# Windowed attention with two MLPs in fp32: when the weights' conversion steps of the 512-token block are traced, and what GpSimd does first

## The chip, the cores and the metric

One core of a Trainium2 chip runs the whole program. The metric is the time of the program on the device in microseconds (us), the median of several runs. The profile is one more execution of the same program, recorded by the hardware profiler.

## The reference

A windowed attention with 4 batches, 8 heads, 576 positions and 64 columns a head, then two MLPs over its 2304 tokens (512 columns, 2048 hidden ones). Only the first MLP matters here:

```python
h = x @ w_in
g = np.where(h >= 1, h, np.where(h <= -1, 0.0, (h + 1) ** 2 / 4))
x = g @ w_out
```

The weights come as float64 and the products have to be nearly exact, so each float32 operand is split into a high and a low part and each product is three matmuls (low x high, high x low, high x high).

## The kernel before

**Stages.** The attention of the first tokens comes first. Then the first MLP goes over the tokens in blocks of 512, 256 and four times 384 tokens, while the attention of later tokens runs in between ("ticks"). The second MLP ends the program. This case is about the first of the blocks, with 512 tokens, which runs from 46.6 us to about 160 us.

**A block.** `run_block` goes over 16 chunks f of 128 hidden columns. `first` (L672) makes h of a chunk in one PSUM bank with 12 matmuls of 512 columns. `activate` makes g of it. `second` (L725) multiplies g with w_out, again 12 matmuls, and is two chunks late (LAG = 2), so that TensorE works on chunk f-2 while g of chunk f is made. From chunk 2 on h has a single PSUM bank, tag h0 (L894 and L895).

**The activation** takes two forms in this block. Even chunks: L712 on VectorE reads h, L713 on ScalarE squares, L714 on VectorE reads h again. Odd chunks: L705 on ScalarE reads h, L706 on ScalarE squares, L707 on VectorE reads h again. Then `split_hi` (L151, ScalarE, "cast of g") makes g's high part and `split_lo` (L158, GpSimd) its low part.

**The weights' conversion.** Float64 weights become float32 with integer arithmetic. The weights of chunk n (tile `raw`) go through three parts:

- part 1, `conv1`: L194 on ScalarE takes the absolute value into tile `m`, L197 on GpSimd leaves the sign in place of the upper words, L198 on ScalarE shifts the lower words
- part 2, `conv2`: L205 on VectorE shifts `m` and sets the sign (it needs L197), L212 on VectorE adds the lower words (it needs L198)
- part 3, `conv3`: L151 on ScalarE makes the high part `wa` ("cast of the weights"), L158 on VectorE the low part; then tile `m` is free. There are two tiles `m`.

Parts 1 and 2 of weights 0 to 2 and part 3 of weights 0 and 1 are traced before the block. The rest is traced by `hook`, which `run_block` calls twice in a chunk: after `first` and `activate` (after = 0), and after `second` (after = 1).

**What sets the order.** A scheduler orders the instructions of each engine by the order of tracing and its own estimate of when each can start; every engine then runs its queue strictly in order. `tc.issue_after(x)` keeps what is traced inside behind x, if it is on the same engine as x. Only SyncE, which issues the DMAs, runs in the order of tracing.

Of the kernel before, what the change touches and what calls it, by code (L numbers as in the profile page):

```python
# [9 lines left out]
F32 = mybir.dt.float32  # L10
# [6 lines left out]
ALU = mybir.AluOpType  # L17
# [13 lines left out]
LO = dict(q="pool", v="pool", x="dve", x_whole="dve", g="pool", g_tail="dve", g2="dve", x2="dve")  # L31
# [11 lines left out]
def tile_window_attention_two_mlps(  # L43
# [76 lines left out]
    def keep_busy(bank, n):  # L120


        for a in range(0, n, 2 * P):
            nc.tensor.matmul(bank[:, a:a + 2 * P], zeros[:, :P], zeros, start=True, stop=True, skip_group_check=True)
# [22 lines left out]
    engines = {"act": nc.scalar, "dve": nc.vector, "pool": nc.gpsimd, "any": nc.any}  # L147

    def split_hi(eng, hi, x):
        if eng == "act":  # L150
            nc.scalar.copy(hi, x)  # L151
        elif eng == "pool":
            nc.gpsimd.tensor_scalar(out=hi, in0=x, scalar1=1.0, scalar2=1.0, op0=ALU.mult, op1=ALU.mult)
        else:
            engines[eng].tensor_copy(hi, x)

    def split_lo(eng, lo, x, hi):
        engines[eng].tensor_tensor(out=lo, in0=x, in1=hi.bitcast(F32), op=ALU.subtract)  # L158

    class Weights:
# [51 lines left out]
        def conv3(self, f):  # L214
            del self.raw[f]
            m = self.m.pop(f)
            hl = wpool.tile([P, 2, 2, PIECE], F32R, tag=f"w{f}", name=f"w{self.nm}{f}")
            split_hi("act", hl[:, 0], m)
            split_lo("dve", hl[:, 1], m, hl[:, 0])
            self.hl[f] = hl  # L220
# [466 lines left out]
    class Mlp1(Mlp):  # L687
# [12 lines left out]
        def activate(self, ps, n):  # L700


            r, g = self.tiles()
            if n == N0 and self.n_first % 2 == 0:
                nc.scalar.activation(out=r[:, :n], in_=ps[:, :n], func=AF.Relu, bias=0.5, scale=0.5)  # L705
                nc.scalar.activation(out=r[:, :n], in_=r[:, :n], func=AF.Square)  # L706
                nc.vector.scalar_tensor_tensor(out=r[:, :n], in0=ps[:, :n], scalar=1.0, in1=r[:, :n],  # L707
                                               op0=ALU.max, op1=ALU.min)
                split_hi(HI["g"], g[:, 0, :n], r[:, :n])
                split_lo(LO[self.g_lo], g[:, 1, :n], r[:, :n], g[:, 0, :n])  # L710
                return g
            nc.vector.tensor_scalar(out=r[:, :n], in0=ps[:, :n], scalar1=-1.0, scalar2=1.0, op0=ALU.max, op1=ALU.min)  # L712
            self.square = nc.scalar.activation(out=r[:, :n], in_=r[:, :n], func=AF.Square, bias=0.5, scale=0.5)  # L713
            self.larger = nc.vector.tensor_tensor(out=r[:, :n], in0=ps[:, :n], in1=r[:, :n], op=ALU.max)  # L714
            split_hi(HI["g"], g[:, 0, :n], r[:, :n])
            split_lo(LO[self.g_lo], g[:, 1, :n], r[:, :n], g[:, 0, :n])
            return g

        def second(self, acc, g, f, n, first, last):
# [118 lines left out]
    W1 = Weights("a", w_in1, w_out1, cpool, True)  # L838
# [12 lines left out]
    def run_block(mlp1, j, part, hook):  # L851
        for f in part:
            chunks.run(mlp1, j, f, part, j, lambda: hook(f, 0), lambda: hook(f, 1), att.behind)

    with ExitStack() as actx:
        mlp1 = Mlp1(W1, blocks1, rpool, GG)
        raw = actx.enter_context(tc.tile_pool(name="raw", bufs=2))
        proc = actx.enter_context(tc.tile_pool(name="proc", bufs=2))
        work = actx.enter_context(tc.tile_pool(name="work", bufs=2))
        dist = actx.enter_context(tc.tile_pool(name="dist", bufs=1)).tile([P, H, 2 * P], BF16, tag="dist", name="dist")  # L860
        zeros = actx.enter_context(tc.tile_pool(name="zeros", bufs=1)).tile([P, 2 * P], BF16, tag="zeros", name="zeros")
        att = Attention(raw, proc, work, XX)

        nc.vector.memset(zeros, 0.0)
        att.clear(range(4))

        nc.scalar.copy(minus_odd, nc.const_aps.tensor(0.0, [P, 1], F32))
        bank = psum.tile([P, BANK], F32, tag="h1", name="busy")
        for _ in range(WARM_UP):
            keep_busy(bank, BANK)  # L870
        make_consts()
        for vt in att.vts:
            nc.gpsimd.memset(vt[:, :, 0:2 * D + 2:2 * D + 1], 1.0)
        att.more_loads(5)

        for t in range(unit_steps[0] + unit_steps[1] + LAG_D + 1):
            att.tick()
            if t < 2:
                with att.behind():
                    att.clear(range(4 + 2 * t, 6 + 2 * t))  # L880
            if t in LOAD_AT:
                W1.load()
            if t in CONV_AT:
                with att.behind(), att.behind_exp():
                    W1.conv_part(CONV_AT[t])

        def spread(ticks):

            slots, att0 = 2 * KF, att.t

            def hook(f, after):
                k = 2 * f + after + 1
                W1.load()
                if f == 1:  # L894
                    mlp1.tags = ("h0",)  # L895
                with att.behind(), att.behind_exp():
                    for part in ((2,) if after else (3, 1)):
                        W1.conv_part(part)
                while att.t < att0 + min(ticks, -(-ticks * k // (slots - 2))):
                    att.tick()  # L900

            return hook

        def even(ticks):

            start = att.t

            n = KF - 1  # L910
            extra = max(0, ticks - n)

            def hook(f, after):
                due = min(n, f + 1) + -(-extra * min(n, f + after) // n)
                while att.t < start + min(ticks, due):
                    att.tick()

            return hook

        mlp1.tags = ("h0", "t2")  # L920
        att.open = False
        ticks = unit_steps[2] + unit_steps[3]
        att.make_tables()
        run_block(mlp1, 0, FULL, spread(ticks))
        assert W1.n_parts == [KF] * 3
        for j in range(1, len(blocks1) - 1):
            ticks = sum(unit_steps[:needs[j + 1]]) + LAG_C_SPLIT - att.t
            run_block(mlp1, j, FULL, even(ticks))
# [246 lines left out]
    for m, blk, f, part, g in chunks.pend:  # L1175
        assert f == KF - 1
        t0, n = m.blocks[blk]
# [181 lines left out]
```

## Time and profile before

| what | us |
|---|---|
| median of 3 runs | 947.78 |
| lowest and highest run | 946.98, 948.83 |
| the profiled execution, its own time | 950.93 |
| its span, first to last instruction | 949.1 |
| TensorE busy in the span | 931.2 |

In the profile PE is TensorE, DVE is VectorE, ACT is ScalarE, POOL is GpSimd and SP is SyncE. L712 is line 712 of the kernel. The granted TensorE clock was 0.998 of full speed over the span. Names such as `wa` or `g` are the program's tiles with the buffer numbers left out.

### The profile page before, as it was taken

Reading aid. Unit: us, or ns where it says so; the run is one execution under the profiler, and the core shown is the slowest. Engines: PE = TensorE matmul, PEld = TensorE weight load, DVE = VectorE, ACT = ScalarE, POOL = GpSimd, SP = SyncE. Lnnn points to the kernel's source line nnn. Section 1 sums busy time; section 2 is a strip of 40 time slices with the busy share of each in tenths; the row PEclk is TensorE's granted clock in tenths of the full one; section 3 lists DMA queues with packets and bytes.
Section 4 is the critical chain, followed back from the end, with each engine's and each line's share of the span. In section 5 each row is a group of like instructions: output and inputs, shape, how many; then the busy total and the mean of one; then the engine's idle time right before and its main releaser. Section 6 shows DMA issues by size and latency. Waiting matters only on the chain.

```text
span 949.1 us, 16367 instructions
## 1 busy us (share of the span) xinstructions
PE 931.2 (98%) x5299; PEld 855.1 (90%) x5299; DVE 653.0 (69%) x1706; ACT 534.4 (56%) x1325; POOL 299.5 (32%) x559
## 2 busy tenths in 40 slices
PE   9999999999999999999999999999999999999998
PEld 7776878999999999999999899999999898988987
DVE  5788785787677677667644899968557777644443
ACT  6887875776666566666534785635333334422232
POOL 2144555887668676777710000000000000000000
PEclk9999999999999999999999999999999999999999
DMA  6675412322222212322008762004264644544431
GB/s 199 205 241 182 164 37 73 96 79 73 74 64 71 81 43 71 91 64 62 1 35 278 251 222 92 1 20 170 78 211 160 239 167 149 174 121 113 122 111 66
DMA packets 92644, 112.73 MB, mean 119 GB/s; under 512 B 8721, under 2 KB 70417, under 8 KB 92561
## 3 DMA queue, kind: packets, MB, share of 16 engines
q1 hardware_dynamic: 92560, 111.71, 36.9%
q8 instruction: 42, 0.69, 0.3%
q14 instruction: 42, 0.34, 0.1%
HBM read 87.56 MB, written 24.12 MB: 118 GB/s over the span
## 4 chain that ended last, share of the span: by engine, by line
PE 74%; DVE 6%; ACT 3%; issue 1%; DMA 1%; POOL 0%; ACTq 0%; SPq 0%; POOLq 0%; DVEq 0%
PE h L672 21%; PE acc L778 21%; PE acc L725 14%; PE y L1260 7%; PE x L1260 5%; PE r L563 3%; PE s L419 2%; PE t L478 1%; DMA rawb<-w_out 1%; DVE kl L399 1%; DVE r L712 1%; DVE ma L212 1%; DVE r L714 1%; DVE x L158 1%; ACT r L713 1%
## 5 line engine op out<-in xcount | busy, mean ns | idle before, releaser
L672 PE MATMUL h<-x,wa 128*128 128x384 f32 (+2 forms) x1152 | 224.4, 341 | 4.9 <-DVE r L714 3.3
L778 PE MATMUL acc<-wb,g 128*128 128x512 f32 x861 | 222.2, 393 | 0.0
L725 PE MATMUL acc<-g,wa 128*128 128x384 f32 (+2 forms) x1152 | 221.9, 339 | 0.0
L672 PEld LDWEIGHTS h<-x,wa 128*128 128x128 f32 x1152 | 191.6, 189 | 16.8 <-DVE r L714 7.4
L725 PEld LDWEIGHTS acc<-g,wa 128*128 128x128 f32 x1152 | 191.7, 189 | 6.3 <-DVE g L158 0.2
L778 PEld LDWEIGHTS acc<-wb,g 128*128 128x128 f32 x861 | 159.4, 188 | 24.9
L151 ACT CAST g<-r 128x384 fp32r<-128x384 f32 (+2 forms) x192 | 98.1, 511 | 68.9 <-DVE r L1207 37.6
L158 POOL TENSOR_TENSOR g<-r,g 128x384 fp32r<-128x384 f32 (+2 forms) x80 | 88.2, 1103 | 57.1 <-ACT g L151 46.6
L158 DVE TENSOR_TENSOR g<-r,g 128x384 fp32r<-128x384 f32 x112 | 62.3, 556 | 41.8 <-ACT g L151 41.4
L713 ACT ACTIVATE r<-r 128x384 f32<-128x384 f32 (+2 forms) x88 | 45.1, 514 | 70.2 <-DVE r L712 70.0
L496 POOL TENSOR_SCALAR_AFFINE_SELECT tt<-dist 128x256 fp32r<-128x256 f32 (+1 forms) x176 | 77.0, 457 | 19.8 <-DVE dist L491 15.3
L712 DVE TENSOR_SCALAR r<-h 128x384 f32<-128x384 f32 (+2 forms) x88 | 47.5, 540 | 41.8 <-PE h L672 33.7
L672 PE MATMUL h<-x,wb 128*128 128x384 f32 x384 | 72.6, 336 | 0.0
L672 PEld LDWEIGHTS h<-x,wb 128*128 128x128 f32 x384 | 68.2, 188 | 2.6
L453 ACT ACTIVATE p<-p,sm 128x128 f32<-128x128 f32 (+2 forms) x134 | 56.7, 429 | 23.9 <-DVE sm L449 23.6
L714 DVE TENSOR_TENSOR r<-h,r 128x384 f32<-128x384 f32 (+2 forms) x88 | 47.8, 544 | 23.5 <-ACT r L713 21.6
L1205 ACT ACTIVATE r<-u 128x384 f32<-128x384 f32 x32 | 16.8, 525 | 56.2 <-DVE u L1269 56.2
L563 PEld LDWEIGHTS r<-tt,vs 128*128 128x128 f32 x304 | 45.1, 189 | 3.5 <-POOL tt L496 1.3
L401 POOL TENSOR_TENSOR qs<-qr,qs 128x256 fp32r<-128x256 f32 (+2 forms) x64 | 39.5, 618 | 26.6 <-ACT qs L398 14.5
L563 PE MATMUL r<-tt,vs 128*128 128x128 f32 (+3 forms) x304 | 44.8, 262 | 1.6 <-POOL tt L496 0.9
L1260 PE MATMUL y<-wb,w 128*128 128x384 f32 x192 | 38.7, 336 | 0.0
L399 DVE SCALAR_TENSOR_TENSOR kl<-kr,kh 128x256 fp32r<-128x256 f32 (+3 forms) x64 | 38.4, 599 | 0.0
(169 smaller groups left out, 1569.2 us busy)
## 6 DMA issues: line engine op xcount, KB each, us to landing
w<-wd SPq DMA_DIRECT2D x88, 256.0 KB, 2.7
rawa<-w_in SPq DMA_DIRECT2D x16, 512.0 KB, 4.8
rawa<-w_out SPq DMA_DIRECT2D x16, 512.0 KB, 5.8
rawb<-w_in SPq DMA_DIRECT2D x16, 512.0 KB, 4.1
rawb<-w_out SPq DMA_DIRECT2D x16, 512.0 KB, 5.0
wd<-sum SPq DMA_DIRECT2D x32, 256.0 KB, 2.1
wd<-wb SPq DMA_DIRECT2D x24, 256.0 KB, 2.8
out<-o SPq DMA_DIRECT2D x17, 256.0 KB, 2.3
```

The lines of the kernel that those rows point to most:

```text
L151: nc.scalar.copy(hi, x)
L158: engines[eng].tensor_tensor(out=lo, in0=x, in1=hi.bitcast(F32), op=ALU.subtract)
L453: self.exp = nc.scalar.activation(out=pt[:, :nk], in_=pt[:, :nk], func=AF.Exp, bias=sm[:, 0:1], scale=-1.0, accum_out=None if u.whole else ...
L496: nc.gpsimd.affine_select(out=u.tt[:, :, s0 + s, :m], in_=both, compare_op=ALU.is_ge, fill=0.0, base=-1 + s, pattern=[[0, 2], [sign, m]], ...
L563: nc.tensor.matmul(u.r[:, qo:qo + nq], u.vs[:, j, c, :, :].rearrange("p a d -> p (a d)"), u.tt[:, part].rearrange("p s q -> p (s q)")[:, s ...
L672: nc.tensor.matmul(ps[:, :n], self.W.w_in(a, c, f), self.x_chunk(x, b, c, n), start=(k == 0), stop=(k == 3 * KC - 1))
L712: nc.vector.tensor_scalar(out=r[:, :n], in0=ps[:, :n], scalar1=-1.0, scalar2=1.0, op0=ALU.max, op1=ALU.min)
L713: self.square = nc.scalar.activation(out=r[:, :n], in_=r[:, :n], func=AF.Square, bias=0.5, scale=0.5)
L714: self.larger = nc.vector.tensor_tensor(out=r[:, :n], in0=ps[:, :n], in1=r[:, :n], op=ALU.max)
L725: nc.tensor.matmul(acc[i][:, o * n:(o + 1) * n], self.W.w_out(a, f)[:, e * P:(e + 1) * P], g[:, b, :n], start=(first and k == 0 and o == 0 ...
L778: nc.tensor.matmul(acc[t][:, :DM], g[:, b, tg * P:(tg + 1) * P], self.W.w_out(a, f), start=(first and k == 0), stop=(last and k == 2))
L1260: nc.tensor.matmul(ps[:, :N2], w[:, a, c * P:(c + 1) * P], self.x.operand(k, c, b), start=(start and n == 0), stop=(n == 5), skip_group_ch ...
```

## The change

`split_lo` returns its instruction, and `activate` keeps that of g's low part as `g_low`. What `hook` traces is held behind `g_low` on GpSimd, which concerns the sign (L197) alone. The parts are traced at other places: from chunk 1 on, the first call of a chunk f has part 2 of weights f+2 and then part 1 of weights f+3, and the second call has part 3 of weights f+2. Before, the first call had part 3 of weights f+2 and part 1 of weights f+3, and the second call part 2 of weights f+3.

```diff
     def split_lo(eng, lo, x, hi):
-        engines[eng].tensor_tensor(out=lo, in0=x, in1=hi.bitcast(F32), op=ALU.subtract)
+        return engines[eng].tensor_tensor(out=lo, in0=x, in1=hi.bitcast(F32), op=ALU.subtract)
...
                 split_hi(HI["g"], g[:, 0, :n], r[:, :n])
-                split_lo(LO[self.g_lo], g[:, 1, :n], r[:, :n], g[:, 0, :n])
+                self.g_low = split_lo(LO[self.g_lo], g[:, 1, :n], r[:, :n], g[:, 0, :n])
                 return g
...
             split_hi(HI["g"], g[:, 0, :n], r[:, :n])
-            split_lo(LO[self.g_lo], g[:, 1, :n], r[:, :n], g[:, 0, :n])
+            self.g_low = split_lo(LO[self.g_lo], g[:, 1, :n], r[:, :n], g[:, 0, :n])
             return g
...
                 W1.load()
                 if f == 1:
                     mlp1.tags = ("h0",)
-                with att.behind(), att.behind_exp():
-                    for part in ((2,) if after else (3, 1)):
-                        W1.conv_part(part)
+                with att.behind(), att.behind_exp(), tc.issue_after(mlp1.g_low.ins):
+                    for part in (3,) if after else (3, 1) if f == 0 else (2, 1):
+                        if not (after and f == 0):
+                            W1.conv_part(part)
```

The order of instructions differs from before on TensorE, VectorE, ScalarE and GpSimd, from chunk 0 or 1 to chunk 15 of this block; behind it, and on SyncE everywhere, it is the same. Three places follow. In the names, `rawa`, `ma` and `wa` with a number are the weights of that chunk; a number behind an underscore only tells buffers apart.

GpSimd, the signs of weights 8 to 10 and the low parts of g of chunks 4 to 7 (`r_1071`, `r_1129`, `r_1204`, `r_1275`), before:

```order
L158 TENSOR_TENSOR g_85<-r_1071,g_85 128x512
L197 TENSOR_SCALAR rawa8_936<-rawa8_936 128x1024
L441 MEMSET p1_115 128x64
L158 TENSOR_TENSOR g_85<-r_1129,g_85 128x512
L441 MEMSET p0_114 128x64
L197 TENSOR_SCALAR rawa9_997<-rawa9_997 128x1024
L158 TENSOR_TENSOR g_85<-r_1204,g_85 128x512
L197 TENSOR_SCALAR rawa10_1077<-rawa10_1077 128x1024
L441 MEMSET p2_116 128x64
L158 TENSOR_TENSOR g_85<-r_1275,g_85 128x512
```

The same stretch now, where the chunks 4 to 7 are `r_1069`, `r_1127`, `r_1202` and `r_1273`:

```order
L158 TENSOR_TENSOR g_85<-r_1069,g_85 128x512
L197 TENSOR_SCALAR rawa7_863<-rawa7_863 128x1024
L441 MEMSET p1_115 128x64
L158 TENSOR_TENSOR g_85<-r_1127,g_85 128x512
L197 TENSOR_SCALAR rawa8_934<-rawa8_934 128x1024
L441 MEMSET p0_114 128x64
L158 TENSOR_TENSOR g_85<-r_1202,g_85 128x512
L197 TENSOR_SCALAR rawa9_995<-rawa9_995 128x1024
L441 MEMSET p2_116 128x64
L158 TENSOR_TENSOR g_85<-r_1273,g_85 128x512
```

The sign of weights 9 stood behind the low part of chunk 5 and now stands behind that of chunk 6; the signs of weights 8 and 10 move by one chunk in the same way.

VectorE, behind the last activation step of chunk 7 (`r_1275`) and around that of chunk 8 (`r_1329`), before:

```order
L707 SCALAR_TENSOR_TENSOR r_1275<-h_1262,r_1275 128x512
L205 SCALAR_TENSOR_TENSOR ma10_1286<-ma10_1286,rawa10_1077 128x1024
L449 ISA p1_115,sm28_1_1312<-s28_1_1310,dist_98 128x192
L449 ISA sm28_1_1312 128x1
L212 ISA ma10_1286<-rawa10_1077,ma10_1286 128x2048
L712 TENSOR_SCALAR r_1329<-h_1316 128x512
L527 TENSOR_SCALAR rec27_1346<-r26_1219 128x4
L449 ISA p2_116,sm29_0_1364<-s29_0_1362,dist_98 128x128
L449 ISA sm29_0_1364 128x1
L158 TENSOR_TENSOR wa10_1337<-ma10_1286,wa10_1337 128x1024
L714 TENSOR_TENSOR r_1329<-h_1316,r_1329 128x512
```

The same stretch now, with chunk 7 as `r_1273` and chunk 8 as `r_1327`:

```order
L707 SCALAR_TENSOR_TENSOR r_1273<-h_1260,r_1273 128x512
L449 ISA p1_115,sm28_1_1310<-s28_1_1308,dist_98 128x192
L449 ISA sm28_1_1310 128x1
L527 TENSOR_SCALAR rec27_1343<-r26_1216 128x4
L528 RECIPROCAL rec27_1343<-rec27_1343 128x4
L158 TENSOR_TENSOR wa9_1300<-ma9_1212,wa9_1300 128x1024
L529 TENSOR_TENSOR y27_1344<-r26_1216,rec27_1343 128x256
L205 SCALAR_TENSOR_TENSOR ma10_1283<-ma10_1283,rawa10_1075 128x1024
L712 TENSOR_SCALAR r_1327<-h_1314 128x512
L212 ISA ma10_1283<-rawa10_1075,ma10_1283 128x2048
L714 TENSOR_TENSOR r_1327<-h_1314,r_1327 128x512
```

L205 of weights 10 stood right behind L707 of chunk 7, with its sign behind the low part of chunk 6; now it stands right ahead of L712 of chunk 8 and its sign behind the low part of chunk 7. L212 now stands between L712 and L714.

ScalarE, from the square of chunk 9 (`r_1407`) to the cast of g, before:

```order
L706 ACTIVATE r_1407<-r_1407 128x512
L194 ACTIVATE ma12_1418<-rawa12_1210 128x1024
L198 ACTIVATE rawa12_1210<-rawa12_1210 128x1024
L151 CAST g_85<-r_1407 128x512
L151 CAST x_78<-x27_1422 128x192
```

The same stretch now (`r_1405`):

```order
L706 ACTIVATE r_1405<-r_1405 128x512
L151 CAST x_78<-x27_1419 128x192
L453 ACTIVATE p1_115<-p1_115,sm30_0_1432 128x128
L151 CAST wa11_1448<-ma11_1337 128x1024
L151 CAST g_85<-r_1405 128x512
```

The conversion of weights 12 no longer stands ahead of the cast of g; the cast of weights 11 does.

## Rows read from the trace of the kernel before

**Rows 1.** The page, busy us by engine, share of the span, instructions.

```profile
PE 931.2 (98%) x5299; PEld 855.1 (90%) x5299; DVE 653.0 (69%) x1706; ACT 534.4 (56%) x1325; POOL 299.5 (32%) x559
```

**Rows 2.** Window: length, busy us of PE, PEld, DVE, ACT, POOL; clock, DMA.

```profile
57.00:160.00 103.00, 99.00 (x493) 78.87 (x493) 81.53 (x155) 78.92 (x144) 53.88 (x54) 1.00 0.43 140
```

**Rows 3.** Waits of TensorE from 57 to 160 us: total, times, longest.

```profile
PE s L419 <- DVE sm L449: 1.1, 2, 0.7
PE h L672 <- DVE r L707: 1.0, 1, 1.0
...
PE h L672 <- DVE r L714: 0.5, 1, 0.5
```

**Rows 4.** Groups by line and shape, 57 to 160 us: busy us, mean ns | idle before.

```profile
L725 PE MATMUL acc<-g,wa 128*128 128x512 f32 x168 | 44.9, 403 | 0.0
L672 PE MATMUL h<-x,wa 128*128 128x512 f32 x168 | 44.3, 403 | 1.9 <-DVE r L707 1.0 <-DVE r L714 0.5 <-DVE sm L456 0.3
...
L212 DVE CUSTOM_DVE_ANT_0 ma<-rawa,ma 128x2048 uint16<-128x2048 uint16 x13 | 22.9, 1765 | 0.3
L197 POOL TENSOR_SCALAR rawa<-rawa 128x1024 f32<-128x1024 f32 x12 | 16.1, 1342 | 14.4 <-ACT ma L194 14.4
...
L151 ACT CAST wa<-ma 128x1024 fp32r<-128x1024 f32 x13 | 13.6, 1044 | 2.4 <-DVE ma L212 1.0 <-DVE rec L527 0.7 <-DVE sm L457 0.7
L151 ACT CAST g<-r 128x512 fp32r<-128x512 f32 x16 | 9.9, 620 | 3.8 <-DVE r L707 2.6 <-DVE r L714 1.1
L707 DVE SCALAR_TENSOR_TENSOR r<-h,r 128x512 f32<-128x512 f32 x8 | 5.5, 684 | 5.6 <-ACT r L706 5.6
L712 DVE TENSOR_SCALAR r<-h 128x512 f32<-128x512 f32 x7 | 4.8, 684 | 1.6 <-PE h L672 1.6
```

**Rows 5.** Timeline of TensorE: first matmuls of h in chunks 4, 14 and 15.

```profile
75.22 1.67 PE L672 MATMUL h<-x,wa 128*128 128x512 f32 x6
...
148.60 3.00 PE L672 MATMUL h<-x,wa 128*128 128x512 f32 x12 [0.32 <-DVE sm L456]
...
154.11 2.91 PE L672 MATMUL h<-x,wa 128*128 128x512 f32 x12
```

**Rows 6.** Timelines of ScalarE, GpSimd and VectorE around that wait, start, us.

```profile
82.73 0.62 ACT L151 CAST g<-r 128x512 fp32r<-128x512 f32 x1
...
83.43 2.04 POOL L158 TENSOR_TENSOR g<-r,g 128x512 fp32r<-128x512 f32 x1 [0.38 <-ACT g L151]
85.43 2.13 POOL L197 TENSOR_SCALAR rawa<-rawa 128x1024 f32<-128x1024 f32 x1
...
84.36 2.19 DVE L212 CUSTOM_DVE_ANT_0 ma<-rawa,ma 128x2048 uint16<-128x2048 uint16 x1
...
87.59 1.23 DVE L205 SCALAR_TENSOR_TENSOR ma<-ma,rawa 128x1024 uint32<-128x1024 uint32 x1 [0.77 <-POOL rawa L197]
88.95 1.23 DVE L212 CUSTOM_DVE_ANT_0 ma<-rawa,ma 128x2048 uint16<-128x2048 uint16 x1
90.10 0.68 DVE L707 SCALAR_TENSOR_TENSOR r<-h,r 128x512 f32<-128x512 f32 x1
```

**Rows 7.** Waits of VectorE from 57 to 160 us: total, times, longest.

```profile
DVE ma L205 <- POOL rawa L197: 4.5, 6, 1.5
```

**Rows 8.** Single lines, 50 to 160 us: duration in ns, minimum/median/maximum.

```profile
L158 POOL TENSOR_TENSOR g<-r,g x16: 1285/1494/2207, 57.5 to 159.9; 128x512 fp32r<-128x512 f32 x16
L158 DVE TENSOR_TENSOR wa<-ma,wa x14: 1207/1225/1226, 52.6 to 146.7; 128x1024 fp32r<-128x1024 f32 x14
...
L197 POOL TENSOR_SCALAR rawa<-rawa x13: 1104/1149/2132, 53.7 to 140.6; 128x1024 f32<-128x1024 f32 x13
L205 DVE SCALAR_TENSOR_TENSOR ma<-ma,rawa x13: 1194/1225/2324, 54.9 to 141.8; 128x1024 uint32<-128x1024 uint32 x13
L212 DVE CUSTOM_DVE_ANT_0 ma<-rawa,ma x13: 1212/1980/2320, 56.6 to 143.1; 128x2048 uint16<-128x2048 uint16 x13
L194 ACT ACTIVATE ma<-rawa x13: 1127/1142/1161, 52.4 to 139.4; 128x1024 f32<-128x1024 f32 x13
```

## Prediction

> **What bounds the kernel now.** I read the busy line first. TensorE is busy 98% of the span [rows 1], so time can come only from its idle stretches, or be lost by new ones. Then the program order of both kernels: they differ only inside the 512-token block of the first MLP, and SyncE's DMA queue is the same in both. So I asked the windows for that block. From 57 us (where the orders part) to 160 us (where the block ends) TensorE is busy 99.0 of 103.0 us [rows 2]: 4.0 us idle, which is the most that any reordering can win. The time that is named goes to few causes: TensorE waits 1.1 us for attention scores, 1.0 us for VectorE's last activation step L707 and 0.5 us for its twin L714 [rows 3].
>
> Why those: from chunk 2 on, h has one PSUM bank. The first matmuls of chunk k+1 (I write h(k+1)) may start only when VectorE has read h(k) for the last time, in L714 (even chunks) or L707 (odd ones). TensorE fills the time with second matmuls (L725) of two chunks earlier and with attention. The block holds 168 + 168 matmuls of 512 columns in these 103 us [rows 4], that is 14 chunks, so TensorE needs 99.0 / 14 = 7.07 us a chunk. If the path from one L714/L707 to the next is longer than 7.07 us, it sets the pace and not TensorE.
>
> The longest single stop, 1.0 us for L707 [rows 3], shows such a path. It is the L707 of chunk 5, at 90.10 us. Ahead of it in VectorE's queue stood L205, which waited for GpSimd's sign (end 85.43 + 2.13 = 87.56, L205 at 87.59), then L212, then L707 [rows 6]. The sign itself stood behind g's low part on GpSimd. Over the block L205 waits 6 times, 4.5 us, for signs [rows 7].
>
> **The change part by part.** Nothing is added or removed: each engine has as many instructions as before. Three things move.
>
> 1. *Signs.* From chunk 5 on, sign k+4 stood behind g's low part of chunk k; now it is sign k+3. Seen from the weights, a sign comes one chunk later on GpSimd. By itself it costs nothing there: GpSimd's wait of 14.4 us in front of signs [rows 4] is the cover.
>
> 2. *Shift and add.* L205 and L212 of weights k+2 now stand right ahead of or between L712 and L714 (before L707) of chunk k, for every k from 1 to 13. In the old order chunks 3, 4, 5 and 6 are tied like this, and chunk 10 as well; elsewhere from chunk 7 on the sign had a whole chunk of slack.
>
> 3. *ScalarE.* The low-part conversion of g gives up its place behind L194/L198 and often stands behind the weights' cast wa instead.
>
> Items 1 and 2 together make a closed path: L714/L707 of chunk k-1, cast of g, g's low part on GpSimd, the sign, L205, L212, L714/L707 of chunk k. Its length from the rows: cast of g 0.62 [rows 4], g's low part alone 1.28 (the minimum), sign 1.15, L205 1.23, L212 1.21 (its minimum) [rows 8], L712 0.68 for even k, and L707 0.68 (L714, over as many columns, is taken alike) [rows 4]. Even: 6.85; odd: 6.17. On one engine a follower starts 0.08 before its predecessor's printed end (88.95 + 1.23 = 90.18, L707 at 90.10), and a hop between engines takes 0.03 (the 87.59 above) to 0.08 (cast of g ends 82.73 + 0.62 = 83.35, GpSimd starts 83.43) [rows 6]. With four or five of the one and three of the other a link loses about 0.19. Bare links, then, are 6.7 and 6.0 us: under 7.07.
>
> What stands in the way on these engines is on top. (a) The low part of the weights (L158, 1.22 us) stands between the sign and L707/L714 in VectorE's queue in the links into chunks 4 and 5, and in the links into 6, 7 and 9 it becomes ready just when the sign starts on GpSimd. Does it then run beside the sign, or wait it out? L205 and L212 took up to 2.32 us, and the pairs of rows show why: g's low part (83.43) and L212 (84.36) finish one after the other, 85.47 and 86.55, and the next sign ends at 87.56 [rows 6]. The low part of the weights itself never took over 1.23 us [rows 8], but never met a GpSimd instruction that had started before it either. Its form is that of L205 (two SBUF operands), so I let it wait: +1.22 in five links, 6.1 us. If it ran beside the sign, the three links 6, 7 and 9 would save about 1.1 each, 3.3 us; that is the lower bound of this term.
> (b) In the links into chunks 8, 10, 11, 12 and 13 the cast of the weights (1.04 [rows 4]) stands ahead of the cast of g on ScalarE. It is released by L212, 0.68 before the link begins, so it delays g by 0.36; and the low part that it releases then holds g's low part for 1.22 - 0.62 = 0.60. About 0.9 a link, 4.5 us. Two links have an attention score row more, 0.5 together.
>
> Sum of the ten links from chunk 3 to chunk 13: 5 x 6.85 + 5 x 6.17 = 65.1, less 1.9, plus 6.1, 4.5 and 0.5: 74.3 us. Before, h(4) to h(14) took 148.60 - 75.22 = 73.38 us [rows 5], in which, counted in the orders, the old one has 118 second matmuls and the new one 116; at 0.24 each (12 take 2.91 [rows 5]) that leaves 72.9. So the path loses 1.4 us there. TensorE's own 70.7 us lie under it.
>
> At the start something comes back: L714 of chunk 0 no longer stands behind L205, so the 0.5 us wait for it [rows 3] goes; ScalarE's L194 now ahead of the first cast of g gives about 0.2 of it back. Behind chunk 13 no weights are left, and h(15) follows as before (154.11 [rows 5]). The buffers of the converted weights are two, so L194 of weights n+2 now waits for the low part of weights n, half a chunk ahead of it: ScalarE time off the path, which I cost at nothing; its price if it isn't covered is the second rival's.
>
> Sum: +1.4 - 0.3, taken as **+1.3 us**. The profiled execution took 950.93 us with a span of 949.1; its span would be 950.4. The median of the runs, 947.78, lies 3.15 below it; the forecast is 947.78 + 1.3 = 949.1.
>
> One rule speaks on the term that I chose. The Trainium skill, "SBUF — State Buffer", section "Who interferes with whom", says that a VectorE instruction with two SBUF inputs and a GpSimd instruction that reads SBUF exclude each other, and the second to issue fully blocks. For L212 against g's low part the trace agrees (2.19 us in place of 1.23, in the pair above). For the low part of the weights no row here shows it; by the rule the sum is +1.3 us, without it -2.0.
>
> **The rivals.** *A, the path is covered, faster.* The low part runs beside the sign or gets in ahead of it; then no link of (a) past chunk 5 is longer than 7.07, and L212 mostly runs alone: 13 times at 1.21 in place of 1.77 [rows 4], 7 us of VectorE that serve the activations. For: L205's 4.5 us of waiting is real and its cure is this order. Against: the links into 4 and 5 keep the low part. Time: 947.78 - 2.0 = 945.8, and with every idle microsecond gone 943.8.
>
> *B, ScalarE lengthens the path, slower.* In the new order L194 or L198 stands ahead of L713, L706 or the cast of g in most chunks. ScalarE is busy 78.92 of 103 us [rows 2], so it often has no gap. I counted none of these. If in three of the ten links one such conversion (1.14 each [rows 8]) lands inside the path, it adds 3.4 us: 949.1 + 3.4 = 952.5. It decides from the point where the path is longer than 7.07 a chunk; below that it costs nothing.
>
> *C, the reordering moves waits only.* TensorE's idle 4.0 us come out again elsewhere: 947.8. That the change does not do what it says is ruled out by the order itself.
>
> **How the numbers follow.** A measurement of this kernel can tell about 0.2%, 1.9 us, from no change. Forecast 0.44, with its own range 947.3 to 950.9 ((a) and (b) are 10.6 us together, which I hold known to about a sixth, 1.8 either way); A 0.24; B 0.20; C 0.12. Faster by over 0.2% is A: 0.24. Slower is B and the upper part of the forecast, above 949.7 (0.16): 0.36. The rest, 0.40, is within 0.2%. For 8 in 10 the range takes in the better part of A and of B: 945.0 to 953.0.
>
> **What would show it.** Right: TensorE's waits for L714 and L707 grow to several us, in chunks 8 to 13 above all; L205's waits for the sign grow or stay although L212 falls to about 1.2 us; the low part of the weights shows instances near 2 us; h(4) comes a little earlier than 75.22 us and h(14) later than 148.60. Wrong: L205 waits for almost no sign, and TensorE's idle time between 57 and 160 us is under 2 us (A); or ScalarE conversions stand in the chain of waits ahead of the cast of g (B).

## The result, and the profile after

| | before | after |
|---|---|---|
| median, us | 947.54 (4 runs) | 953.22 (4 runs) |
| lowest and highest run, us | 946.98, 948.83 | 952.02, 953.69 |
| the profiled execution, own time and span, us | 950.93, 949.1 | 953.69, 952.0 |

The change is **slower**: the ratio after to before is 1.0057, with a 95% interval from 1.0044 to 1.0069, which is 5.4 us (4.2 to 6.5). The forecast was 949.1 us, +1.3, with 945.0 to 953.0 us for 8 in 10; the measured median, 953.22, lies 0.2 us above the upper end.

The busy line of the page after, which answers to [rows 1], hardly moves:

```profile
PE 929.7 (98%) x5299; PEld 854.1 (90%) x5299; DVE 648.7 (68%) x1706; ACT 535.3 (56%) x1325; POOL 303.1 (32%) x559
```

The window from 57 to 160 us of after, which answers to [rows 2], shows where the time goes. TensorE is now idle 9.0 us there, not 4.0:

```profile
57.00:160.00 103.00, 94.04 (x468) 75.10 (x467) 76.99 (x150) 76.62 (x140) 57.08 (x53) 1.00 0.41 133
```

The waits of TensorE in the same stretch of after (in total, times, longest) answer to [rows 3]:

```profile
PE h L672 <- DVE r L714: 3.9, 4, 1.2
PE h L672 <- DVE r L707: 3.8, 6, 1.0
```

1.5 us of waits for VectorE's last activation steps have become 7.7 us, ten of them in one block. The wait of VectorE that answers to [rows 7]:

```profile
DVE ma L205 <- POOL rawa L197: 18.5, 12, 2.8
```

So L205 now waits for nearly every sign. The groups by form of after, 57 to 160 us, answer to [rows 4]:

```profile
L158 POOL TENSOR_TENSOR g<-r,g 128x512 fp32r<-128x512 f32 x15 | 22.7, 1517 | 42.3 <-ACT g L151 31.5 <-issue 10.8
L197 POOL TENSOR_SCALAR rawa<-rawa 128x1024 f32<-128x1024 f32 x13 | 19.2, 1478 | 0.0
L158 DVE TENSOR_TENSOR wa<-ma,wa 128x1024 fp32r<-128x1024 f32 x13 | 17.2, 1321 | 3.3 <-ACT wa L151 3.1
L212 DVE CUSTOM_DVE_ANT_0 ma<-rawa,ma 128x2048 uint16<-128x2048 uint16 x13 | 16.6, 1280 | 0.0
```

L212 fell from 1765 to 1280 ns a piece, as, in all but one instance (2.04 us), it no longer meets g's low part, and GpSimd's 14.4 us of idle time in front of signs is gone: the sign stands right behind g's low part every time. L212 costs VectorE 6.3 us less (22.9 against 16.6), and yet TensorE lost 5.0.

TensorE's timeline of after, first matmuls of h in chunks 4 and 14 (in [rows 5] 75.22 and 148.60):

```profile
74.56 1.66 PE L672 MATMUL h<-x,wa 128*128 128x512 f32 x6 [1.04 <-DVE r L707]
...
151.89 0.96 PE L672 MATMUL h<-x,wa 128*128 128x512 f32 x3 [0.79 <-DVE r L707]
```

From h(4) to h(14) it takes 77.33 us, where it took 73.38. The block's last chunk follows, and the next block's first matmul comes at 163.93 us in place of 159.57, 4.4 us later. Behind that the orders are the same; the distance grows by another 0.5 us up to 250 us and then stays near 4.9 us to 500 us.

**One link of the path.** From L714 of chunk 6 to L707 of chunk 7 in after, ScalarE, GpSimd, VectorE and TensorE:

```profile
97.28 0.68 DVE L714 TENSOR_TENSOR r<-h,r 128x512 f32<-128x512 f32 x1
98.00 0.62 ACT L151 CAST g<-r 128x512 fp32r<-128x512 f32 x1 [0.89 <-DVE r L714]
98.77 1.30 POOL L158 TENSOR_TENSOR g<-r,g 128x512 fp32r<-128x512 f32 x1 [4.31 <-ACT g L151]
99.95 1.23 DVE L158 TENSOR_TENSOR wa<-ma,wa 128x1024 fp32r<-128x1024 f32 x1 [0.65 <-ACT wa L151]
100.03 2.10 POOL L197 TENSOR_SCALAR rawa<-rawa 128x1024 f32<-128x1024 f32 x1
102.17 1.23 DVE L205 SCALAR_TENSOR_TENSOR ma<-ma,rawa 128x1024 uint32<-128x1024 uint32 x1 [1.00 <-POOL rawa L197]
103.43 1.23 DVE L212 CUSTOM_DVE_ANT_0 ma<-rawa,ma 128x2048 uint16<-128x2048 uint16 x1
104.57 0.68 DVE L707 SCALAR_TENSOR_TENSOR r<-h,r 128x512 f32<-128x512 f32 x1
...
105.31 0.72 PE L672 MATMUL h<-x,wa 128*128 128x512 f32 x2 [0.50 <-DVE r L707]
```

It is the forecast's closed path, step by step, with no gap over 0.15 us. The low part of the weights started 0.08 us ahead of the sign, and the sign took 2.10 us in place of 1.15: of the 1.15 us that the low part still had to run, 0.95 came on top of the sign, so that the two ran nearly one after the other. The link takes 104.57 - 97.28 = 7.29 us, and TensorE, done early, waits the last 0.50.

### The profile page after: what moved, and what is told of

It reads as the page before. It is cut to its first block, busy times and chain, and to the rows that moved or that the text cites. A ratio compares the mean times of both kernels' runs of the same rounds, so it can differ in the third digit from the quotient of the medians.

```text
span 952.0 us, 16357 instructions
## 1 busy us (share of the span) xinstructions
PE 929.7 (98%) x5299; PEld 854.1 (90%) x5299; DVE 648.7 (68%) x1706; ACT 535.3 (56%) x1325; POOL 303.1 (32%) x559
## 4 chain that ended last, share of the span: by engine, by line
PE 74%; DVE 5%; ACT 2%; issue 2%; DMA 1%; POOL 1%; SPq 0%; ACTq 0%; POOLq 0%; DVEq 0%
PE h L672 21%; PE acc L778 21%; PE acc L725 14%; PE y L1261 7%; PE x L1261 5%; PE r L563 3%; PE s L419 2%; PE t L478 1%; DVE kl L399 1%; DVE r L712 1%; DMA rawb<-w_out 1%; DVE r L714 1%; DVE x L158 1%; DMA x2r<-x2d 0%; ACT vs L151 0%
## 5 line engine op out<-in xcount | busy, mean ns | idle before, releaser
L712 DVE TENSOR_SCALAR r<-h 128x384 f32<-128x384 f32 (+2 forms) x88 | 47.5, 540 | 39.4 <-PE h L672 31.5
L714 DVE TENSOR_TENSOR r<-h,r 128x384 f32<-128x384 f32 (+2 forms) x88 | 47.8, 544 | 23.9 <-ACT r L713 22.2
L401 POOL TENSOR_TENSOR qs<-qr,qs 128x256 fp32r<-128x256 f32 (+2 forms) x64 | 40.2, 630 | 27.0 <-ACT qs L398 15.1
L399 DVE SCALAR_TENSOR_TENSOR kl<-kr,kh 128x256 fp32r<-128x256 f32 (+3 forms) x64 | 39.0, 609 | 0.0
```

Source lines behind the costliest of these rows:

```text
L399: nc.vector.scalar_tensor_tensor(out=u.kl[:, :nk], in0=u.kr[:, :nk], scalar=unit, in1=u.kh[:, :nk].bitcast(F32), op0=ALU.mult, op1=ALU.sub ...
```

## The experiments

Two theories went to the chip first. **Theory 1**: the closed path through the sign sets the pace. **Theory 2**: ScalarE's new order (rival B of the forecast) lengthens each activation. The time of each run is a median; the ratio is to the kernel before on the same chip, with its 95% interval. "End" is the first matmul of the next block in the profile, 159.57 us before and 163.93 after; the block itself begins at 46.0 to 46.7 us in all profiles but one, which is named below.

**The signs alone.** The old places of tracing, with the one rule that holds what the hook traces behind g's low part (`g_low` kept as in the change):

```diff
-                with att.behind(), att.behind_exp():
+                with att.behind(), att.behind_exp(), tc.issue_after(mlp1.g_low.ins):
                     for part in ((2,) if after else (3, 1)):
                         W1.conv_part(part)
```

> The signs are held behind g's low part, but the parts are traced as before the change. Theory 1: the sign of weights k+3 stands behind the low part of chunk k, and in the order L205 of k+2 stands ahead of L714/L707 of chunk k almost everywhere, so the path is closed as in the change: 951 to 954, and L205 waits over 12 us for signs. Theory 2: the tracing is the old one, so 947.5 within 2 us.

Measured: 955.39 us, ratio 1.0083 (1.0070 to 1.0097), end 167.44. The wait of L205 in this kernel:

```profile
DVE ma L205 <- POOL rawa L197: 22.9, 11, 3.2
```

The links from chunk 3 to chunk 8 are a metronome, 7.63, 7.17, 7.64, 7.17, 7.66 us: that is a closed path, with the even ones, which have L712 in them, 0.47 longer. Two links, into chunks 9 and 12, take 10.3 us: there the low part of the weights, too, stands between the late L212 and L707 or L714. The signs' place alone costs more than the whole change does, with ScalarE's conversions traced where they were before. Theory 1 holds so far.

**The path cut.** The change as it is, with VectorE's conversion steps also held behind L714/L707 of their chunk, so that L205 can wait for a sign without an activation behind it:

```diff
-                nc.vector.scalar_tensor_tensor(out=r[:, :n], in0=ps[:, :n], scalar=1.0, in1=r[:, :n],
+                self.larger = nc.vector.scalar_tensor_tensor(out=r[:, :n], in0=ps[:, :n], scalar=1.0, in1=r[:, :n],
...
-                with att.behind(), att.behind_exp(), tc.issue_after(mlp1.g_low.ins):
+                with att.behind(), att.behind_exp(), tc.issue_after(mlp1.g_low.ins), tc.issue_after(mlp1.larger.ins):
```

> The whole change, and in addition the weights' steps on VectorE that are traced in a chunk (L205, L212, the low part) are held behind that chunk's last activation step, L714 or L707. The signs stay behind g's low part. Theory 1: nothing that waits for a sign stands ahead of the activation of the same chunk any more, the path is open, and the time is that of before or a little less, 945 to 949. Theory 2: ScalarE's places change little, so 951 to 954.

Measured: 947.08 us, ratio 0.9994 (0.9984 to 1.0003), end 159.51. The whole loss is gone, with the same rule on the signs and with ScalarE's conversions traced where the change has them. The groups of L205 and of the low part of the weights in this kernel:

```profile
L158 DVE TENSOR_TENSOR wa<-ma,wa 128x1024 fp32r<-128x1024 f32 x14 | 20.8, 1487 | 4.0 <-ACT wa L151 3.9
...
L205 DVE SCALAR_TENSOR_TENSOR ma<-ma,rawa 128x1024 uint32<-128x1024 uint32 x13 | 15.8, 1213 | 0.0
```

L205 waits for no sign at all. On ScalarE a conversion still makes the cast of g late in eight of the ten links from chunk 3 to 13, by 0.20 to 0.55 us (in the change in six, by 0.44 to 0.48), and here that costs nothing. Theory 2 falls as the main cause.

**The tracing alone**, without the rule on the signs:

```diff
-                with att.behind(), att.behind_exp(), tc.issue_after(mlp1.g_low.ins):
+                with att.behind(), att.behind_exp():
                     for part in (3,) if after else (3, 1) if f == 0 else (2, 1):
```

> The parts are traced as in the change, but the signs are not held behind g's low part. In the resulting order the sign of weights k+4 stands right behind g's low part of chunk k again, as before the change, while shift and add keep their new places. Theory 1 (the path L714/L707, cast of g, g's low part, sign, L205, L212, L714/L707 closes because of the sign's place and sets the pace): the sign has a chunk of slack again, L205 waits for signs under 6 us in all and not 18.5, and the time is that of before, 947.5 within 2 us. Theory 2 (ScalarE: the tracing puts the cast of the weights ahead of the cast of g and lets L194 wait for the low part of the weights): those places stay, and the time stays at 952 to 954.

Measured: 949.93 us, ratio 1.0030 (1.0018 to 1.0041), end 161.14; L205 waits 3.1 us for signs, 4 times. It isn't quite the no-change that Theory 1 allowed for. Its largest single stop, on GpSimd, VectorE and TensorE in order of time:

```profile
112.22 1.56 POOL L158 TENSOR_TENSOR vs<-vr,vs 128x192 fp32r<-128x192 f32 x1
113.74 1.72 POOL L401 TENSOR_TENSOR qs<-qr,qs 128x256 fp32r<-128x256 f32 x1
115.43 1.11 POOL L197 TENSOR_SCALAR rawa<-rawa 128x1024 f32<-128x1024 f32 x1
116.57 1.23 DVE L205 SCALAR_TENSOR_TENSOR ma<-ma,rawa 128x1024 uint32<-128x1024 uint32 x1 [1.50 <-POOL rawa L197]
117.72 0.35 DVE L158 TENSOR_TENSOR x<-x,x 128x192 fp32r<-128x192 f32 x1
118.21 0.45 PE L478 MATMUL t<-ident,p 128*128 128x128 f32 x1 [2.79 <-DVE x L158]
```

Attention's own steps (`vs`, `qs`) stood ahead of the sign on GpSimd, the sign came 1.5 us late for L205, and behind L205 stood attention's `x`, for which TensorE's queue stopped 2.79 us. The windows of the same kernel around it (the last but two column is the granted clock) show that the stop cost more than itself:

```profile
116.00:118.00 2.00, 0.00 (x0) 0.00 (x0) 1.43 (x3) 0.61 (x1) 0.54 (x1) 0.92 0.00 0
118.00:120.00 2.00, 1.79 (x5) 1.53 (x6) 2.00 (x4) 1.30 (x3) 0.54 (x1) 0.50 0.00 0
120.00:122.00 2.00, 2.00 (x8) 1.55 (x8) 2.00 (x1) 0.54 (x1) 0.94 (x1) 0.73 0.00 0
```

Behind the empty 2 us the clock was granted at 0.50, its lower level, and the h of that chunk took 3.53 us where it takes 2.9.

**The signs one chunk earlier.** The change, with a sign held behind g's low part of the chunk before:

```diff
+                if not after:
+                    low.append(mlp1.g_low)
-                with att.behind(), att.behind_exp(), tc.issue_after(mlp1.g_low.ins):
+                with att.behind(), att.behind_exp(), tc.issue_after(low[max(0, len(low) - 2)].ins):
```

> The whole change, but the sign is held behind the low part of the chunk before, so that it may go one chunk earlier. Theory 1: as with free signs, 947.5 within 2 us, L205 waits under 6 us. Theory 2: 951 to 954.

Measured: 951.17 us, ratio 1.0037 (1.0024 to 1.0049), end 163.31, with 3.1 us of waits of L205 for signs. It loses where the run before loses too: link 4 takes 9.5 us in both and link 12 takes 10.2. There L205, L212 and the low part stand one behind the other in front of L712 or L714, without much waiting for signs. The groups of L212 and L205 in this kernel:

```profile
L212 DVE CUSTOM_DVE_ANT_0 ma<-rawa,ma 128x2048 uint16<-128x2048 uint16 x13 | 23.8, 1831 | 0.1
L205 DVE SCALAR_TENSOR_TENSOR ma<-ma,rawa 128x1024 uint32<-128x1024 uint32 x13 | 20.4, 1567 | 3.1 <-POOL rawa L197 3.1
```

In the change they take 1280 and 1252 ns. By its number this run goes with Theory 2 and not with Theory 1; by L205's waits, under 6 us, it goes with Theory 1. So the two parts of the change do not add up: the new places of tracing alone cost some 3 us, the signs' place alone 8, both together 5.4. With the signs behind g's low part VectorE waits for them; without that it meets g's low part and is stretched, as before.

**The cut path without the rule on the signs.** On TensorE, VectorE and ScalarE this kernel and the one with the path cut stand in the same order, instruction by instruction.

```diff
-                with att.behind(), att.behind_exp(), tc.issue_after(mlp1.g_low.ins), tc.issue_after(mlp1.larger.ins):
+                with att.behind(), att.behind_exp(), tc.issue_after(mlp1.larger.ins):
```

> The kernel in which VectorE's conversion steps are held behind L714/L707 of their chunk (947.08 us), without the rule on the signs. Its orders on TensorE, VectorE and ScalarE are the same instruction by instruction; only GpSimd's signs come ahead of g's low part where they can. Theory 1 (the closed path through the sign is what costs): once L205 stands behind L714/L707 the path is open and the sign's place is worth nothing, 947.1 within 1.2 us, and L205 waits for signs under 1.5 us in the block. Theory 2 (the signs' place costs by itself, through g's low part coming later or earlier on GpSimd): the time follows the place as it did between the change and its variant without the rule, 3.3 us less, 943.8.

Measured: 947.21 us, ratio 0.9991 (0.9981 to 1.0000), end 158.19. It is the cleanest pair here: the same rule on the signs is worth nothing when L205 stands behind the activation, and 3.3 us when it stands ahead of it (953.22 against 949.93; 2.6 us by the two ratios). The Theory 2 of this expectation is another one, that the signs' place costs by itself; its number, 943.8, is missed.

**Shift and add alone behind the activation**, the low part left to the scheduler (`larger` kept as in the cut path above):

```diff
-                            W1.conv_part(part)
+                            with ExitStack() as held:
+                                if part == 2:
+                                    held.enter_context(tc.issue_after(mlp1.larger.ins))
+                                W1.conv_part(part)
```

> The change, with L205 and L212 alone held behind L714/L707 of their chunk; the low part of the weights (L158) goes where the scheduler puts it. Theory 1 (L205 behind the sign closes the path, the low part only adds to it): the path is open, 947.1 within 1.5 us, no wait of L205 for signs over 1.5 us in all. Theory 3 (the low part of the weights in VectorE's queue is what costs, 6.1 us by the forecast's term, whether or not the path is closed): about half of the loss stays where it can stand ahead of L714/L707, 950 or more.

Measured: 948.01 us, ratio 1.0000 (0.9989 to 1.0011), no wait of L205 for signs. A low part still stands in each of the links 3 to 13, and up to 2.14 us long. Theory 3 falls: the low part in VectorE's queue does not cost by itself.

**Half of the low part.**

```diff
-            split_lo("dve", hl[:, 1], m, hl[:, 0])
+            if self.sign_pool and 3 <= f <= 13:
+                split_lo("dve", hl[:, 1, 0], m[:, 0], hl[:, 0, 0])
+            else:
+                split_lo("dve", hl[:, 1], m, hl[:, 0])
...
+            if self.sign_pool and 3 <= f <= 13:
+                part = 0
             return self.hl[f][:, part, 1, :]
```

> The change, with the low part of the weights 3 to 13 made for w_in alone (the low part of w_out is left out, and TensorE multiplies with the high part in its place): 512 of 1024 columns, about 0.61 us less in each. The closed path stays. Forecast's terms: the low part was to cost 1.22 in five links and 0.60 in five more by holding g's low part; half of it takes 0.61 from each of the five and all of the 0.60 from most of the others, 3 to 6 us less than the change: 947 to 950 us, h(4) to h(14) 71.5 to 74.5 us in place of 77.3. Theory 4 (the excess over the forecast, attention's steps against the sign and the wait for a free tile m, is most of the loss): under 2 us less, 951.3 or more.

Measured: 951.63 us, ratio 1.0037 (1.0024 to 1.0050), 1.6 us less than the change, which is Theory 4's number; as the two intervals overlap, the links say more. Those into chunks 5 to 9 take 6.73, 7.29, 6.81, 7.17 and 7.22 us, against 7.26, 7.79, 7.29, 7.64 and 7.67 in the change: 0.45 to 0.53 less in every one. The low part and the sign of link 7:

```profile
101.11 0.69 DVE L158 TENSOR_TENSOR wa<-ma,wa 128x512 fp32r<-128x512 f32 x1 [0.83 <-ACT wa L151]
...
101.20 1.61 POOL L197 TENSOR_SCALAR rawa<-rawa 128x1024 f32<-128x1024 f32 x1
```

The sign falls from 2.10 to 1.61 us with the instruction that it waits out. So the forecast's term for the low part is right in kind, and nearly in size (0.49 where 0.61 was to go). Link 12, though, takes 10.04 us in this kernel (8.41 in the change): L205 waits for a sign there with attention's `kl` (L399) ahead of it, L212 now stands in front of L712, and a second low part, not halved, stands in front of L714. That gives back 1.6 us, so the ten links take 75.2 us, more than the expectation's 74.5.

**The sign off GpSimd**, on the change:

```diff
-    W1 = Weights("a", w_in1, w_out1, cpool, True)
+    W1 = Weights("a", w_in1, w_out1, cpool, False)
```

> The change with the sign of the first MLP's weights made on VectorE (the program's other form: a shift and a masked or in place of L205, one instruction more for each of 16 weights) and none on GpSimd. Theory 1: no path through GpSimd is left; VectorE has about 0.7 to 1.2 us more work a chunk, and where it stands ahead of L714/L707 and the attention's steps it can cost again: 946 to 950 us, with links under 7.5 us on average. Rival (VectorE's order is the loss, the sign not): the loss stays and the added VectorE work comes on top, 953 to 965.

Measured: 949.12 us, ratio 1.0021 (1.0010 to 1.0033), end 159.94; the ten links take 71.76 us. VectorE has the 14.8 us of a further instruction to do, in an order that is not quite the change's, and most of the loss is still gone. In the block itself all of it is: the block begins at 47.88 us here (46.60 before) and takes 112.06 us to its end (112.97 before). It is the sign on GpSimd, and not VectorE's load, that made the links long.

**The sign twice**, in the change and in the cut path. The second one changes nothing in the data:

```diff
-                nc.gpsimd.tensor_scalar(out=sign, in0=sign, scalar1=0.0, scalar2=1.0, op0=ALU.mult, op1=ALU.mult)
+                for _ in range(2 if 4 <= f <= 13 else 1):
+                    nc.gpsimd.tensor_scalar(out=sign, in0=sign, scalar1=0.0, scalar2=1.0, op0=ALU.mult, op1=ALU.mult)
```

> The change, with the sign (L197) of weights 4 to 13 done twice on GpSimd (the second finds zeros with the right sign and changes nothing): 1.1 us more GpSimd work in each of ten chunks, on an engine that is busy 55% of the block. Theory 1 (the sign lies on a closed path that sets the pace): every link from chunk 3 to 11 grows by about 1.1 us, some less where a wait was in it already; 8 to 11 us more than the change, 961 to 964 us, and L205 waits for signs near 28 us in the block in place of 18.5. Rival (GpSimd has room and the loss comes from VectorE's or ScalarE's order): within 1.5 us of the change, 952 to 955.

> The same doubled signs in the kernel whose VectorE conversion steps stand behind L714/L707 of their chunk (947.08 us with single signs). The instructions stand in the same order there. Theory 1: the path is open, so the extra 11 us of GpSimd work are covered; what is left is that L205, L212 or the low part of the weights wait out a longer GpSimd instruction: 947 to 949 us. Rival (the extra work costs wherever it stands, by holding VectorE): 8 us or more, as in the change.

Measured: 958.63 us in the change (ratio 1.0116, 1.0098 to 1.0133), 5.4 more; 953.07 us in the cut path (1.0060, 1.0042 to 1.0078), 6.0 more. Both numbers miss Theory 1's, in opposite directions, and the second one tells something new. The low part of the weights and L205 with the path cut and signs doubled (lines are one further down in this kernel):

```profile
L158 DVE TENSOR_TENSOR wa<-ma,wa 128x1024 fp32r<-128x1024 f32 x14 | 24.0, 1714 | 4.4 <-ACT wa L151 4.4
...
L206 DVE SCALAR_TENSOR_TENSOR ma<-ma,rawa 128x1024 uint32<-128x1024 uint32 x13 | 17.2, 1322 | 1.8 <-POOL rawa L198 1.8
```

L205 still waits for almost no sign. But the low part of the weights went from 1487 to 1714 ns: it waits out the longer GpSimd work, and it stands in front of the next chunk's L714 or L707. One link, into chunk 11, takes 11.3 us, 2.5 more than with single signs: most of L205's wait, 1.6 us, falls there, TensorE stops 2.73 us for attention's scores behind it, and the granted clock of the 2 us from 132 us on is 0.52. Cutting the path takes away nearly all of the wait for the sign, not the exclusion. As the doubled signs cost about the same in both kernels, this pair does not tell the theories apart. In the change, in turn, L205's waits stayed at 18.4 us: the links into the odd chunks 5 to 13 grew by 1.0 to 2.1 us, those into the even ones from 6 on didn't, as the scheduler now put L712 ahead of L205 in chunks 6, 8, 10 and 12.

**The old tracing, held.** The kernel before, with the same rule (`larger` kept as above):

```diff
-                with att.behind(), att.behind_exp():
+                with att.behind(), att.behind_exp(), tc.issue_after(mlp1.larger.ins):
                     for part in ((2,) if after else (3, 1)):
```

> The kernel before, its tracing kept, with the hook's VectorE steps held behind L714/L707 of their chunk. Theory 1: the old order's sign waits (4.5 us, of which 1.0 reached TensorE) go, TensorE's idle 4.0 us shrink a little: 946.5 within 1.5 us. Rival: part 2 of weights k+3 is now tied to the second half of chunk k, the low part of weights k+2 stands behind L714/L707 of chunk k and in front of the next chunk's, and TensorE waits for it as often: 948 to 950.

Measured: 956.27 us, ratio 1.0086 (1.0070 to 1.0101), end 167.64, outside both numbers. TensorE's waits there:

```profile
PE t L478 <- DVE x L158: 3.8, 4, 1.7
PE s L419 <- DVE sm L449: 3.7, 4, 1.4
PE h L672 <- DVE r L707: 2.1, 2, 1.2
```

In the old tracing part 2 of weights k+3 and part 3 of weights k+2 then come on VectorE in one heap behind the same L707, signs come beside them, and the low part takes 2.31 to 2.33 us three times from 57 to 97 us, beside g's low part; attention's `x` and its score rows stand behind the heap, and TensorE waits for those. The rule that cures the change spoils the kernel before.

**The kernel before, profiled again.**

> The kernel before, for a second profile of it, because the one shown has a clock of 0.98 between 500 and 600 us and took 950.9 us where the median is 947.8. Expected of both theories: time 947.5 within 1.5 us, the stretch from 57 to 160 us as before (TensorE busy 99 of 103 us), a clock of 1.00 from 500 to 600 us, and so a span about 3 us shorter.

Measured: 947.37 us, span 945.5. Its stretch from 520 to 560 us, and behind it that of the profile shown of before:

```profile
520.00:560.00 40.00, 39.10 (x224) 38.35 (x223) 35.59 (x53) 32.39 (x45) 0.00 (x0) 1.00 0.75 262
```

```profile
520.00:560.00 40.00, 38.18 (x210) 37.50 (x209) 34.98 (x51) 31.01 (x43) 0.00 (x0) 0.96 0.72 250
```

The first profile of before had a dip of the clock there, far behind the block, and that is most of why its span and that of after lie only 2.9 us apart. Against the second one the spans differ by 6.5 us and the ends of the block by 163.93 - 158.57 = 5.36. Of these 0.56 us stood before the block began (46.59 and 46.03 us), where the kernels are alike, so the block is 4.8 us longer by this profile and 4.4 by the first; with the 0.5 us behind it that is 4.9 to 5.3, within the interval of the runs.

No version beats the kernel before: the best three (947.08, 947.21, 948.01) are equal to the kernel before within their intervals.

## Why the prediction was right, and where it was not

**The sign was right and the mechanism was right.** The path that it named (activation, cast of g, g's low part, sign, L205, L212, activation) is there row by row; it is what sets the pace (signs alone: +7.9 us; path cut: nothing left; sign off GpSimd: most of it gone). The size was too small, +1.3 in place of +5.4, and the measured median lies just outside the stated range. Nor did the chances favour this end: no change within 0.2% had 0.40 and slower had 0.36. The forecast said of the signs' new place that it costs nothing by itself, under the cover of GpSimd's 14.4 us of waiting; with the old tracing that place alone cost 7.9 us, as the later sign closes a path there too.

**The sum.** +1.4 - 0.3 is 1.1, which was taken as 1.3 with no reason given. From the first profile of before, its parts are -0.3 (start), +0.92 (74.3 - 73.38, the links) and +0.48 (two matmuls' worth behind chunk 13). Measured they are -0.66, +3.95 and +1.07, together the 4.36 us by which the block ends later.

**The term that was mis-sized** is the sum of the ten links, 74.3 us, which measured 77.33:

| link into chunk | 4 | 5 | 6 | 7 | 8 | 9 | 10 | 11 | 12 | 13 | sum |
|---|---|---|---|---|---|---|---|---|---|---|---|
| forecast | 7.88 | 7.20 | 7.88 | 7.20 | 7.56 | 7.45 | 7.56 | 7.13 | 7.56 | 6.88 | 74.3 |
| measured | 8.41 | 7.26 | 7.79 | 7.29 | 7.64 | 7.67 | 8.09 | 7.63 | 8.41 | 7.14 | 77.33 |

The forecast row is worked out by its own steps: 6.85 or 6.17 less 0.19, plus 1.22 or 0.9, plus the score rows. The links into chunks 5 to 8 are within 0.1 us, in part by luck: in link 7 the low part lengthened the sign by 0.95 us where 1.22 was added, and the steps' starts cost 0.13 us where 0.19 was taken off. Of the excess of 3.0 us 2.4 sits in four others, with these rows in the profile of after:

```profile
72.68 1.22 DVE L158 TENSOR_TENSOR wa<-ma,wa 128x1024 fp32r<-128x1024 f32 x1
73.93 1.14 ACT L194 ACTIVATE ma<-rawa 128x1024 f32<-128x1024 f32 x1 [1.21 <-DVE wa L158]
74.98 0.60 ACT L151 CAST g<-r 128x512 fp32r<-128x512 f32 x1
...
121.60 1.22 DVE L158 TENSOR_TENSOR wa<-ma,wa 128x1024 fp32r<-128x1024 f32 x1
121.77 2.20 POOL L158 TENSOR_TENSOR g<-r,g 128x512 fp32r<-128x512 f32 x1 [4.41 <-ACT g L151]
...
138.98 0.66 DVE L399 SCALAR_TENSOR_TENSOR kl<-kr,kh 128x384 fp32r<-128x384 f32 x1
139.19 1.43 POOL L197 TENSOR_SCALAR rawa<-rawa 128x1024 f32<-128x1024 f32 x1
140.58 2.09 POOL L158 TENSOR_TENSOR vs<-vr,vs 128x192 fp32r<-128x192 f32 x2
140.65 1.59 DVE L205 SCALAR_TENSOR_TENSOR ma<-ma,rawa 128x1024 uint32<-128x1024 uint32 x1 [1.01 <-POOL rawa L197]
```

- Link 4 (+0.53): L194 waited 1.21 us for a free tile `m`, that is for the low part that ended at 73.90, and the cast of g stood behind it, ready since L707 ended. The forecast had named this wait and costed it at nothing, as off the path; its price was half a microsecond, once. A third tile `m` was not tried.
- Link 10 (+0.53): the low part held g's low part for 2.20 - 1.28 = 0.92 us, where step (b) had 0.60; the cast of g was 0.44 us late, where it had 0.36.
- Links 11 and 12 (+0.50, +0.85): attention. `kl` on VectorE held the sign (1.43 us for 1.15, and 1.44 in link 11), and `vs` on GpSimd held L205 (1.59 for 1.23). The forecast counted attention's score rows in the links, and none of its steps that exclude others on these two engines. This is the step that failed most; the rows name about 0.9 of the 1.35 us.

**What else held.** Term (a): in links 4 and 5 the low part stands on VectorE between the sign and the activation's last step, and in links 6, 7 and 9 it and the sign exclude each other, with the sign (2.10 to 2.14 us) as the one that waits; half the low part took 0.45 to 0.53 out of each of the links 5 to 9. Term (b): in links 8, 10, 11, 12 and 13, and in no others, the cast of the weights makes the cast of g late. The rule of the Trainium skill, "SBUF — State Buffer", section "Who interferes with whom", on which the forecast stood against its own lower bound, agrees with that in the main: 2.10 us for the sign behind a low part that began 0.08 earlier, 1.61 behind half of it, though the sign's 0.95 us are not the whole 1.15 that a full block would add. The start: h(4) came 0.66 us earlier (0.64 against the second profile, both counted from the block's first matmul), where 0.3 was forecast. "L205's waits grow although L212 falls": 18.5 us and 1280 ns.

**What did not.** Low parts near 2 us were forecast; only one came (2.18 us), since it was the low part that started first and the sign that waited. Behind chunk 13 the block took 12.78 us to its end in place of 11.71; of these 1.07 the forecast had 0.5, as matmuls pushed behind.

**The rivals.** A (covered) fell: TensorE idles 9.0 us, not under 2. C (waits only move) fell with it. B (ScalarE lengthens the path) had the number nearest to the result, 952.5, but not the cause: of its three conversions in the path one is found, L194 in link 4, and with the path cut ScalarE's conversions cost nothing.

**What stays open.** Why the new tracing alone loses 2.5 to 3.5 us is read from two profiles (links 4 and 12) and not tested apart; nor are the 0.5 us of links 9 and 13 (in link 9 attention's `qs`, L401, held g's low part on GpSimd for 0.4 us after its cast was done), the 0.6 us behind chunk 13 and the 0.5 us behind the block.

## What to carry to other kernels

When a step is moved, look for a path that comes back to its own start one round later (here: activation, GpSimd, VectorE, activation), add up its length for one round and compare that with what the busiest engine needs for a round; a queue that looks idle on average is no cover for it. Add to such a sum the other stages' steps on the same engines, and the waits for free tiles, as they stand in the order; the sum without them was 4% too low here, and that was more than half of the loss. The cure is to put the waiting step behind the one that must not wait, but it has to be tried in the order at hand: the same rule took the whole loss away in one order and cost 8 us in another.

## What was not expected of the hardware

Of a pair of instructions that exclude each other, the one that starts second pays for most of what the first has still to run: the sign took 2.10 us in place of 1.15 behind a low part that began 0.08 us earlier, the low part up to 2.33 us in place of 1.22 beside g's low part, and 1.61 us was left of the sign's 2.10 when the low part was halved. This carries a load on GpSimd into VectorE's path without any dependency: 11 us more of signs cost 6.0 us with the path cut, 2.5 of it in the one link in which L205 did wait for a sign. And a single stop of TensorE of 2.8 us was followed by a granted clock of 0.50 in the next 2 us, with 3.53 us for 12 matmuls that take 2.9.
